# The last 64 channels of an MLP computed with tokens on partitions, and the last output tile stored in three parts

## The chip, the cores and the metric

One core of a Trainium2 chip runs the whole program. The metric is the device time in microseconds (us) of one execution. The profiler's span is 1.3 to 1.6 us shorter than the time that the same execution is given.

## The reference

A transformer block with adaptive modulation: attention with 32 heads over a cache of 2048 keys, then a gated sub-block whose MLP has 1728 inner channels. Only that MLP is touched.

```python
# x: (1, 2048, 640); w3: (640, 1728); w4: (1728, 640)
h = _gelu(_layernorm(x, axis=-1) @ w1)
hs = jnp.concatenate([g0, g1, g2, g3], axis=-1) @ w2   # g0..g3: quarters of h, shifted along the tokens
x1 = x + hs
h2 = _gelu(_layernorm(x1, axis=-1) @ w3) @ w4
return x1 + h2
# and outside:
x = x + gb * _B_ref(h, B_w1, B_w2, B_w3, B_w4)
```

1728 is 13 x 128 + 64, so the last tile of inner channels is half full.

## The kernel before

The program is written as a list of operations. A scheduler with a cost model puts them in order on each engine, and the result is one fixed instruction stream per engine. It decides with this line how long an engine is taken:

```python
t_eng[e] = s + (o.dur if o.dma else max(o.dur - self.LAP.get(e, 0.0), 60.0))
```

The W3 product puts 128 inner channels on partitions and 512 tokens in the free dimension; the 14th tile is padded with zero weights. W4 then takes gelu's output as the stationary operand, 128 tokens at a time.

```python
def w3_part(ch, key):
    for f in range(NF):                        # NF = 14
        m = Tile(pool="T")
        for kk in range(KT):                   # KT = 5
            P.op("PE", ... matmul(m.ap, w3_ap[:, kk, f * 128:(f + 1) * 128], nT_ap[ch][:, kk, :], ...)   # 128 x 512
        P.op("ACT", ... activation(gT_ap[:, f, :], m.ap, GELU) ...)

def w4_tile(t, key):
    for hf in range(2):                        # two column halves of 320
        for f in range(NF):
            P.op("PE", ... matmul(m[:, hf * 512:hf * 512 + HD], gT_ap[:, f, i * 128:(i + 1) * 128],
                                  w4_ap[f][:, hf * HD:(hf + 1) * HD], ...)
        if last:                               # the last tile: each half is finished and stored by itself
            P.op("DVE", ... tensor_tensor(out=w[:, c0:c1], in0=m[...], in1=mod_t[5][:, c0:c1], op=ALU.mult) ...)
            P.op("DVE", ... tensor_tensor(out=o_[:, c0:c1], in0=w[:, c0:c1], in1=b[:, c0:c1], op=ALU.add) ...)
            dma("SP", ... dma_start(out2d[t * 128:(t + 1) * 128, c0:c1], o_[:, c0:c1]) ...)
```

The zeros are written by two fills, whose place in the order is set by a priority (`E + 12` is that of a stage near the end of attention, where the cache buffers under W3 and W4 come free):

```python
pad, pad2 = T(), T()
P.op("POOL", lambda e: e.memset(w3_ap[:, :, FF:FP], 0.0), 300, (), (pad,), E + 12, over=kv(2, 3, 4))
P.op("DVE", lambda e: e.memset(w4_ap[NF - 1][FL:128, :], 0.0), 400, (), (pad2,), E + 12, slack=500.0, over=kv(4))
```

In the same stretch the MLP's input is normalised. Here the vector engine reads two operands from SBUF (the on-chip memory that holds these tiles), while GpSimd does other multiplies and adds of the same stage:

```python
P.op("DVE", lambda e, ...: e.scalar_tensor_tensor(            # "the centring"
    out=b.ap, in0=x1[t].ap, scalar=mv_ap[g1][:, i, 0:1], in1=mod_t[4][:], op0=ALU.subtract, op1=ALU.mult), ...)
...
tt("POOL", b.ap, b.ap, mod_t[3][:], ALU.add, ...)
```

## Time and profile before

| | before |
|---|---|
| time, median of 3 runs (range) | 1368.05 us (1367.85 to 1371.74) |
| last query projection but one to first W1 matmul | 26.58 us (1170.47 to 1197.05) |
| first W1 to first W3 matmul | 30.28 us |
| W3 and W4 stretch, first W3 to end of last matmul | 139.10 us |
| last matmul to last vector instruction, and on to the end | 1.05 and 1.82 us |

The segments come from the trace in order of time. The first W3 matmul of the kernel before is missing from its trace; its start is taken as 0.216 us ahead of the first one recorded. The marker at 1170.47 is the last query projection but one (one more begins 11.31 us later). The page gives the span to 0.1 us, so every length that is reckoned to the end of the run, here and in the tables below, is good to 0.05 us only. A row has the start in us, the duration in us, the engine (SPq is the queue that issues transfers), the line, the operation, output and inputs, shapes, a count, and in brackets the idle time before it with what ended it.

GpSimd in order of time, near the end of attention:

```profile
1177.15 1.56 POOL L538 TENSOR_TENSOR f_y<-f_y,f_mod 128x640 f32<-128x640 f32 x1
1178.66 1.54 POOL L538 TENSOR_TENSOR f_hT<-f_tmp,f_y 128x640 bf16<-128x640 f32 x1
1181.30 0.36 POOL L921 MEMSET f_KV<- 128x320 bf16 x1 [1.10 <-PE f_O L825]
1182.70 1.54 POOL L538 TENSOR_TENSOR f_hT<-f_tmp,f_y 128x640 bf16<-128x640 f32 x1 [1.03 <-DVE f_rl L832]
```

The vector engine in order of time, the same microseconds:

```profile
1178.98 1.91 DVE L861 SCALAR_TENSOR_TENSOR f_y<-f_hT,f_small,f_mod 128x640 f32<-128x640 bf16 x1
1182.82 0.33 DVE L922 MEMSET f_KV<- 64x320 uint32 x1
...
1187.14 0.86 DVE L861 SCALAR_TENSOR_TENSOR f_y<-f_hT,f_small,f_mod 128x640 f32<-128x640 bf16 x1
```

GpSimd works without a break until 1180.20. Then its fill has to wait 1.10 us for the matmuls that still read the buffer. One centring lasts 1.91 us where its peers last 0.86: it starts at 1178.98.

### The profile page before, as it was taken

What the parts mean: (1) busy time and instruction counts of PE and PEld (TensorE: products, weight loads), DVE (VectorE), ACT (ScalarE), POOL (GpSimd) and SP (SyncE); (2) the same over time, 40 slices, a digit from 0 to 9 for tenths busy, and PEclk for the clock granted to TensorE, in tenths of its full rate; (3) what the DMA queues carried; (4) which work ended last, traced back from release to release, by engine and by line L of the source; (5) the groups of instructions that cost most, each with busy time, mean ns of one, the idle gap of its engine ahead of it and who ended that gap; (6) DMA issues with size and microseconds to landing.
All of it is one profiled execution on the core that took longest, in us unless ns stands there. A gap on an engine that the chain in (4) does not pass through costs nothing.

```text
span 1369.3 us, 29631 instructions
## 1 busy us (share of the span) xinstructions
PE 1349.0 (99%) x12841; PEld 939.4 (69%) x13075; DVE 574.7 (42%) x1440; ACT 1103.3 (81%) x1145; POOL 111.7 (8%) x97
## 2 busy tenths in 40 slices
PE   8999999999999999999999999999999999999999
PEld 6666777677677777677677777776776776655665
DVE  5554344544323332332333233233233345799553
ACT  6988888888888888888888888888888888833322
POOL 1000000000000000000000000000233237500000
PEclk9999999999999999999999999999999999999999
DMA  9642614272335221241205121422236110441210
GB/s 211 144 97 36 115 40 81 34 130 59 81 65 90 55 48 35 48 89 33 58 10 101 36 47 36 91 54 48 55 63 136 27 15 19 114 84 44 40 43 31
DMA packets 264787, 90.38 MB, mean 66 GB/s; under 512 B 244793, under 2 KB 262266, under 8 KB 264650
## 3 DMA queue, kind: packets, MB, share of 16 engines
q1 hardware_dynamic: 260682, 84.17, 30.9%
q0 software_dynamic: 672, 2.56, 0.9%
q10 hardware_dynamic: 3296, 1.67, 0.6%
q8 instruction: 104, 1.70, 0.5%
q14 instruction: 33, 0.27, 0.1%
HBM read 41.68 MB, written 2.63 MB: 32 GB/s over the span
## 4 chain that ended last, share of the span: by engine, by line
PE 96%; DMA 1%; issue 1%; DVE 1%; ACT 0%; POOL 0%; SPq 0%; POOLq 0%
PE f_O L825 35%; PE f_S L806 29%; PE f_M L729 10%; PE f_M L760 10%; PE f_S L1002 2%; PE f_M L1002 2%; PE f_O L989 2%; PE f_S L989 2%; PE f_S L940 1%; PE f_S L963 1%; PE f_M L963 1%; DMA f_KV<-in_A_v_cache_dram 1%; PE f_O L940 1%; DMA f_W<-in_w_mod_dram 1%; PE f_O L760 0%
## 5 line engine op out<-in xcount | busy, mean ns | idle before, releaser
L808 ACT ACTIVATE f_PQ<-f_S 128x1024 bf16<-128x1024 f32 x1024 | 1042.6, 1024 | 137.5 <-PE f_S L806 105.0
L825 PEld LDWEIGHTS f_O<-f_KV,f_PQ 128*128 128x128 bf16 x8192 | 634.8, 98 | 262.3 <-DVE f_small L517 1.4
L825 PE MATMUL f_O<-f_KV,f_PQ 128*128 128x129 bf16 x8192 | 796.4, 220 | 9.3 <-DMA f_KV<-in_A_v_cache_dram 0.9
L806 PE MATMUL f_S<-f_PQ,f_KV 128*128 128x512 bf16 x1831 | 650.8, 379 | 3.2 <-DMA f_KV<-in_A_k_cache_dram 0.7
L768 DVE TENSOR_TENSOR f_y<-f_M,f_y 128x320 f32<-128x320 f32 x192 | 94.4, 492 | 465.5 <-PE f_M L760 465.5
L760 PE MATMUL f_M<-f_wo,f_OO 128*128 128x320 bf16 x992 | 272.9, 299 | 0.0
L806 PEld LDWEIGHTS f_S<-f_PQ,f_KV 128*128 128x128 bf16 x2048 | 191.6, 98 | 13.4 <-ACT f_PQ L808 2.2
L729 PE MATMUL f_M<-f_hT,f_wq 128*128 128x512 bf16 (+1 forms) x635 | 189.0, 378 | 1.8 <-DVE f_tmp L771 0.2
L760 PEld LDWEIGHTS f_M<-f_wo,f_OO 128*128 128x128 bf16 x992 | 96.3, 98 | 28.5
L834 DVE TENSOR_TENSOR f_OO<-f_O,f_rl 128x256 bf16<-128x256 f32 x256 | 108.4, 423 | 8.3
L538 POOL TENSOR_TENSOR f_y<-f_y,f_mod 128x640 f32<-128x640 f32 x32 | 49.2, 1544 | 735.2 <-DVE f_y L768 735.1
L733 DVE CAST f_PQ<-f_M 128x512 bf16<-128x512 f32 x127 | 87.8, 692 | 50.7 <-PE f_M L729 49.5
L729 PEld LDWEIGHTS f_M<-f_hT,f_wq 128*128 128x128 bf16 x640 | 62.5, 98 | 49.8 <-DVE f_tmp L771 0.6
L832 DVE RECIPROCAL f_rl<-f_O 128x2 f32<-128x2 f32 x256 | 43.5, 170 | 69.1 <-PE f_O L825 58.2
L992 ACT ACTIVATE f_OO<-f_S 128x512 bf16<-128x512 f32 x28 | 16.7, 597 | 43.6 <-PE f_S L989 43.6
L766 DVE COPY f_y<-f_M 128x320 f32<-128x320 f32 x32 | 15.7, 492 | 57.6 <-PE f_M L760 57.6
L499 DVE BATCH_NORM_STATS2 f_small<-f_y 128x6 f32<-128x320 f32 (+1 forms) x72 | 32.3, 479 | 1.0 <-POOL f_y L538 0.9
L1002 PE MATMUL f_S<-f_KV,f_OO 128*128 128x320 bf16 x224 | 31.7, 299 | 0.0
L1002 PE MATMUL f_M<-f_KV,f_OO 128*128 128x320 bf16 x224 | 31.7, 299 | 0.0
L544 ACT ACTIVATE f_xn<-f_y,f_small 128x640 bf16<-128x640 f32 x10 | 9.1, 916 | 25.7 <-DVE f_small L523 25.7
L661 DVE TENSOR_REDUCE f_small<-f_tmp 128x1 f32<-128x640 f32 x20 | 16.4, 820 | 29.9 <-ACT f_PQ L808 29.9
L992 ACT ACTIVATE f_OO<-f_O 128x512 bf16<-128x512 f32 x28 | 16.7, 596 | 14.1 <-PE f_O L989 14.1
(148 smaller groups left out, 534.9 us busy)
## 6 DMA issues: line engine op xcount, KB each, us to landing
f_KV<-in_A_v_cache_dram SPq DMA_DIRECT2D x28, 512.0 KB, 4.7
f_wo<-in_A_wo_dram SPq DMA_DIRECT2D x8, 640.0 KB, 4.3
f_wq<-in_A_wq_dram SPq DMA_DIRECT2D x7, 640.0 KB, 4.9
f_xin<-in_A_x_dram SPq DMA_DIRECT2D x13, 320.0 KB, 3.5
out_dram<-f_xin SPq DMA_DIRECT2D x15, 160.0 KB, 1.8
f_KV<-in_B_w_dram SPq DMA_DIRECT2D x5, 432.0 KB, 3.6
f_KV<-in_A_k_cache_dram SPq DMA_TRANSPOSE x128, 2.7
f_OO<-f_OO SPq DMA_TRANSPOSE x128, 2.5
```

The source lines that it names most:

```text
L538: P.op(eng, lambda e: e.tensor_tensor(out=out, in0=a, in1=b, op=op), COST[eng][0], rd, wr, prio, lat=300 if eng == "POOL" else None, dual= ...
L729: P.op("PE", lambda e, i=i, kk=kk, mm=mm, a=a, z=z: e.matmul(mm[:, 0:z - a], wq_t[g % 2][:, kk, hh * 128:(hh + 1) * 128], hT_t[ch][:, kk, ...
L733: P.op("DVE", lambda e: e.tensor_copy(q.ap, m.ap), 690, (m,), (q,), s * NP - 90)
L760: P.op("PE", lambda e, m=m, qt=qt, hf=hf, hh=hh: e.matmul(m[:, 0:HD], OT_ap[gs][:, qt, hh, :], wo_t[g % 2][:, hh, hf * HD:(hf + 1) * HD], ...
L768: P.op("DVE", lambda e, m=m, yt=yt: e.tensor_tensor(out=yt.ap, in0=m[:, 0:HD], in1=yt.ap, op=ALU.add), 490, (m, yt), (yt,), s * NP - 60)
L806: P.op("PE", lambda e, sp=sp, r=r, kt=kt: e.matmul(sp[:, r * QC:(r + 1) * QC], K_ap[b][:, kt * 128:(kt + 1) * 128], q.ap, start=True, stop ...
L808: x = P.op("ACT", lambda e, sp=sp, pt=pt: e.activation(pt.ap.rearrange("p k q -> p (k q)"), sp.ap, ACT.Exp, scale=SCALE), 1021, (sp,), (pt ...
L825: ins = e.matmul(o[bk][:, w * 129:w * 129 + 129], pt[:, r, qt * 128:(qt + 1) * 128], V_ap[b][:, u, 0:129], start=(u == 0 and w == 0), stop ...
L832: P.op("DVE", lambda e, ov=ov, i0=i0: e.reciprocal(rl_t[:, i0:i0 + 2].unsqueeze(2), ov[:, 0:258].rearrange("p (u d) -> p u d", u=2)[:, :, ...
L834: evac.append(P.op("DVE", lambda e, ov=ov, i0=i0, bk=bk: e.tensor_tensor(out=On_ap[gs][:, 2 * bk:2 * bk + 2, hh, :], in0=ov[:, 0:258].rear ...
L989: P.op("PE", lambda e, m=m, f=f, kk=kk: e.matmul(m.ap, w3_ap[:, kk, f * 128:(f + 1) * 128], nT_ap[ch][:, kk, :], start=(kk == 0), stop=(kk ...
L1002: P.op("PE", lambda e, f=f, hf=hf: e.matmul(m[:, hf * 512:hf * 512 + HD], gT_ap[:, f, i * 128:(i + 1) * 128], w4_ap[f][:, hf * HD:(hf + 1) ...
```

## The change

The intent is to stop computing the 64 padded channels, and to shorten what follows the last matmul. The last 64 channels are computed with tokens on partitions (64 columns instead of a full 128 x 512 tile), gelu is applied, and a DMA transpose turns them. Two token tiles share one turned tile, so W4 gets a second copy of its last weights, with the zeros in the other half. The last output tile is finished in parts of 320, 192 and 128 columns. The scheduler may now let matrix operations last less than 60 ns.

```diff
@@ the scheduler
-            t_eng[e] = s + (o.dur if o.dma else max(o.dur - self.LAP.get(e, 0.0), 60.0))
+            t_eng[e] = s + (o.dur if o.dma or e == "PE" else max(o.dur - self.LAP.get(e, 0.0), 60.0))
@@ the fills
-    pad, pad2 = T(), T()
-    P.op("POOL", lambda e: e.memset(w3_ap[:, :, FF:FP], 0.0), 300, (), (pad,), E + 12, over=kv(2, 3, 4))
-    P.op("DVE", lambda e: e.memset(w4_ap[NF - 1][FL:128, :], 0.0), 400, (), (pad2,), E + 12, slack=500.0, over=kv(4))
... (cut: the old load of the last weights)
+    w4b = T(), T()
+    for i in range(2):
+        w = w4_ap[NF - 1 + i]
+        P.op("POOL", lambda e, w=w: e.memset(w, 0.0), 700, (), (w4b[i],), 3000, over=kv(4))
+        dma("SP", lambda e, i=i, w=w: e.dma_start(w[i * FL:(i + 1) * FL, :], B_w4[(NF - 1) * 128:FF, :]), 80, (), (w4b[i],), E + 10)
@@ w3_part
+        m = Tile(pool="T")
+        for kk in range(KT):
+            for i in range(4):
+                c0 = (i % 2) * 128 + (i // 2) * FL
+                P.op("PE", ... e.matmul(m[:, c0:c0 + FL], nT_ap[ch][:, kk, i * 128:(i + 1) * 128], w3_ap[:, kk, FN * 128:FF], ...)
+        P.op("ACT", lambda e, m=m: e.activation(gl_ap, m[:, 0:256], GELU), act(256), (m,), (gl,), key, over=old)
+        dmaT(lambda e: e.dma_start_transpose(gT_ap[:, FN, 0:256].rearrange("p (k q) -> p k q", k=2), gl_ap), 64, (gl,), (gT[FN],), key, over=old)
-        for f in range(NF):
+        for f in range(FN):                                  # 13 full tiles
@@ w4_tile
-        for hf in range(2):
+        if last:
+            m3 = Tile(pool="T")
+            parts = ((m, 0, 0, HD), (m, 512, HD, 512), (m3, 0, 512, D))
+        else:
+            parts = ((m, 0, 0, HD), (m, 512, HD, D))
... (cut: the loops over these parts)
```

One thing moves beside what the words name: both fills are now GpSimd's, at priority 3000, so behind the additions of that stage.

More of the change, by code (lines that the diff above doesn't have):

```diff
@@ L287, in fast_path @@
     FL = FF - (NF - 1) * 128
-    FP = NF * 128
+    FN = NF - 1
     G4 = D // 4
@@ L360, in fast_path @@
     gT = [T() for _ in range(NF)]
+    gl_ap = gT_ap[:, NF - 1, 256:512]
+    gl = T()
     wq = [[T() for _ in range(HG)] for _ in range(2)]
@@ L379, in fast_path @@
     W3_OFF = 2 * KVW
-    w3_ap = KV_t[:, W3_OFF:W3_OFF + KT * FP].rearrange("p (k n) -> p k n", k=KT)
+    w3_ap = KV_t[:, W3_OFF:W3_OFF + KT * FF].rearrange("p (k n) -> p k n", k=KT)
     w3 = [T() for _ in range(KT)]
-    W4_HI = W3_OFF + KT * FP
+    W4_HI = W3_OFF + KT * FF
     NW4 = 12
-    w4_ap = [KV_t[:, f * D:(f + 1) * D] for f in range(NW4)] + [KV_t[:, W4_HI + f * D:W4_HI + (f + 1) * D] for f in range(NF - NW4)]
+    w4_ap = [KV_t[:, f * D:(f + 1) * D] for f in range(NW4)] + [KV_t[:, W4_HI + f * D:W4_HI + (f + 1) * D] for f in range(NF + 1 - NW4)]
     w4 = [T() for _ in range(3)]
     w4_of = lambda f: w4[0] if f < 6 else (w4[1] if f < NW4 else w4[2])
-    assert NW4 * D <= W3_OFF and W4_HI + (NF - NW4) * D <= NKV * KVW
+    assert NW4 * D <= W3_OFF and W4_HI + (NF + 1 - NW4) * D <= NKV * KVW and FL == 64
     MM = lambda n: n / 2.4 + 2.5
@@ L910, in fast_path @@
     for k, old in ((0, kv(2)), (1, kv(2)), (2, kv(2, 3)), (3, kv(3)), (4, kv(3, 4))):
-        dma("SP", lambda e, k=k: e.dma_start(w3_ap[:, k, 0:FF], B_w3[k * 128:(k + 1) * 128, :]), 432, (), (w3[k],), E + 5 + k, over=old)
+        dma("SP", lambda e, k=k: e.dma_start(w3_ap[:, k, :], B_w3[k * 128:(k + 1) * 128, :]), 432, (), (w3[k],), E + 5 + k, over=old)
     for i, (f0, f1, old) in enumerate(((0, 6, kv(0)), (6, 12, kv(0, 1)))):
@@ L916, in fast_path @@
     dma("SP", lambda e: e.dma_start(w4_ap[NF - 2], B_w4[(NF - 2) * 128:(NF - 1) * 128, :]), 160, (), (w4[2],), E + 10, over=kv(4))
-    w4b = T()
-    dma("SP", lambda e: e.dma_start(w4_ap[NF - 1][0:FL, :], B_w4[(NF - 1) * 128:FF, :]), 80, (), (w4b,), E + 10, over=kv(4))
-    pad, pad2 = T(), T()
-    P.op("POOL", lambda e: e.memset(w3_ap[:, :, FF:FP], 0.0), 300, (), (pad,), E + 12, over=kv(2, 3, 4))
-    P.op("DVE", lambda e: e.memset(w4_ap[NF - 1][FL:128, :], 0.0), 400, (), (pad2,), E + 12, slack=500.0, over=kv(4))
+    w4b = T(), T()
[3 more added lines that the diff above has]
+        dma("SP", lambda e, i=i, w=w: e.dma_start(w[i * FL:(i + 1) * FL, :], B_w4[(NF - 1) * 128:FF, :]), 80, (), (w4b[i],), E + 10)
     DEL = [1, -1, 2, -2]
@@ L985, in w3_part @@
     def w3_part(ch, key):
-        for f in range(NF):
+        old = tuple(a for b in On + OT for a in b) if ch == 0 else ()
+        m = Tile(pool="T")
+        for kk in range(KT):
+            for i in range(4):
+                c0 = (i % 2) * 128 + (i // 2) * FL
+                P.op("PE", lambda e, m=m, kk=kk, i=i, c0=c0: e.matmul(m[:, c0:c0 + FL], nT_ap[ch][:, kk, i * 128:(i + 1) * 128], w3_ap[:, kk, FN * 128:FF],
+                                                                     start=(kk == 0 and i == 0), stop=(kk == KT - 1), skip_group_check=True),
+                     MM(FL) + 4, (w3[kk], nT[ch][i]), (m,), key + 0.1 * kk + 0.01 * i, accum=True)
+        P.op("ACT", lambda e, m=m: e.activation(gl_ap, m[:, 0:256], GELU), act(256), (m,), (gl,), key, over=old)
+        dmaT(lambda e: e.dma_start_transpose(gT_ap[:, FN, 0:256].rearrange("p (k q) -> p k q", k=2), gl_ap), 64, (gl,), (gT[FN],), key, over=old)
+        for f in range(FN):
             m = Tile(pool="T")
@@ L990, in w3_part @@
                                                                     start=(kk == 0), stop=(kk == KT - 1)),
-                     MM(QC), (w3[kk], pad) + tuple(nT[ch]), (m,), key + f + 0.1 * kk, accum=True)
+                     MM(QC), (w3[kk],) + tuple(nT[ch]), (m,), key + 1 + f + 0.1 * kk, accum=True)
             P.op("ACT", lambda e, m=m, f=f: e.activation(gT_ap[:, f, :], m.ap, GELU),
-                 act(QC), (m,), (gT[f],), key + f, over=tuple(a for b in On + OT for a in b) if ch == 0 else ())
+                 act(QC), (m,), (gT[f],), key + 1 + f, over=old)
     def w4_tile(t, key):
@@ L999, in w4_tile @@
         last = t == SQ // 128 - 1
-        for hf in range(2):
+        if last:
[3 more added lines that the diff above has]
+            parts = ((m, 0, 0, HD), (m, 512, HD, D))
+        for n, (mm, o, c0, c1) in enumerate(parts):
             for f in range(NF):
-                P.op("PE", lambda e, f=f, hf=hf: e.matmul(m[:, hf * 512:hf * 512 + HD], gT_ap[:, f, i * 128:(i + 1) * 128],
-                                                                 w4_ap[f][:, hf * HD:(hf + 1) * HD], start=(f == 0), stop=(f == NF - 1)),
-                     MM(HD), (gT[f], w4_of(f), w4b, pad2), (m,), key + hf + 0.01 * f, accum=True)
+                P.op("PE", lambda e, f=f, mm=mm, o=o, c0=c0, c1=c1: e.matmul(mm[:, o:o + c1 - c0], gT_ap[:, f, (i % 2 if f == FN else i) * 128:][:, 0:128],
+                                                                             w4_ap[f + i // 2 if f == FN else f][:, c0:c1], start=(f == 0), stop=(f == NF - 1)),
+                     MM(c1 - c0), (gT[f],) + ((w4b[i // 2],) if f == FN else (w4_of(f),)), (mm,), key + n + 0.01 * f, accum=True)
             if last:
-                c0, c1 = hf * HD, (hf + 1) * HD
-                w, o_ = tmp[t % 2], xin[3 * hf]
-                P.op("DVE", lambda e, hf=hf, c0=c0, c1=c1: e.tensor_tensor(out=w[:, c0:c1], in0=m[:, hf * 512:hf * 512 + HD], in1=mod_t[5][:, c0:c1], op=ALU.mult),
-                     490, (m, mod[5][hf]), (w,), key - 1000)
-                P.op("DVE", lambda e, o_=o_, c0=c0, c1=c1: e.tensor_tensor(out=o_[:, c0:c1], in0=w[:, c0:c1], in1=b[:, c0:c1], op=ALU.add), 490, (w, b), (o_,), key)
+                w, o_ = tmp[t % 2], xin[(0, 3, 1)[n]]
+                P.op("DVE", lambda e, mm=mm, o=o, c0=c0, c1=c1: e.tensor_tensor(out=w[:, c0:c1], in0=mm[:, o:o + c1 - c0], in1=mod_t[5][:, c0:c1], op=ALU.mult),
+                     dve(c1 - c0), (mm,) + tuple(mod[5]), (w,), key - 1000)
+                P.op("DVE", lambda e, o_=o_, c0=c0, c1=c1: e.tensor_tensor(out=o_[:, c0:c1], in0=w[:, c0:c1], in1=b[:, c0:c1], op=ALU.add),
+                     dve(c1 - c0), (w, b), (o_,), key)
                 dma("SP", lambda e, o_=o_, c0=c0, c1=c1: e.dma_start(out2d[t * 128:(t + 1) * 128, c0:c1], o_[:, c0:c1]), 80, (o_,), (), key)
```

## The prediction

> **What bounds the kernel now.** I read the page first, then the chain that ended last over the closing part, then the matrix engine in order of time, then the head (where small matmuls can be seen alone), then the last six microseconds. The page gives the engine shares:
>
> ```profile
> PE 1349.0 (99%) x12841; PEld 939.4 (69%) x13075; DVE 574.7 (42%) x1440; ACT 1103.3 (81%) x1145; POOL 111.7 (8%) x97
> PE 96%; DMA 1%; issue 1%; DVE 1%; ACT 0%; POOL 0%; SPq 0%; POOLq 0%
> ```
>
> The first line is busy time; the second is the chain of waits that ends the run. Both say the matmul stream is the limit, with the clock at 1.00 throughout. The diff touches only the MLP at the end, so what counts is whether that stretch is also matmul-bound. The chain from the fourth W3 chunk to the end (start, length, what):
>
> ```profile
> 1336.16 2.10 PE f_S L989 x9
> 1338.26 2.16 PE f_O L989 x10
> ...
> 1358.82 3.80 PE f_M L1002 x28
> 1362.62 3.82 PE f_S L1002 x28
> 1366.44 0.02 issue
> 1366.46 0.50 DVE f_tmp L1008
> 1366.97 0.02 issue
> 1366.99 0.49 DVE f_xin L1010
> ```
>
> Line 989 is the W3 product, line 1002 the W4 product. They follow each other with no gap, so time taken off a matmul there moves everything behind it. Ten 512-column matmuls take 2.16 us, so one is 0.216 us; 28 320-column ones take 3.80 us, so one is 0.136 us. (The missing tenth record at 1336 is lost, not a wait: 9 x 0.216 is only 1.94 us.) After the last matmul only a multiply, an add and the store remain.
>
> Small matmuls, each with a full 128x128 weight load of its own, are visible in two places: the modulation columns in the head and the attention's PV products. In order of time (start, length, engine):
>
> ```profile
> 9.29 0.65 PE L465 MATMUL f_M<-f_s_bf,f_W 128*128 128x1 bf16 x20 [0.16 <-DMA f_W<-in_w_mod_dram]
> 9.28 0.56 PEld L465 LDWEIGHTS f_M<-f_s_bf,f_W 128*128 128x128 bf16 x20 [0.30 <-DMA f_W<-in_w_mod_dram]
> 1177.59 0.66 PEld L825 LDWEIGHTS f_O<-f_KV,f_PQ 128*128 128x128 bf16 x8
> 1177.80 0.62 PE L825 MATMUL f_O<-f_KV,f_PQ 128*128 128x129 bf16 x8
> ```
>
> A record of a matmul includes its drain (0.16 us for one column, the mean of that group; 0.22 us for 129). So 20 one-column matmuls start (0.65 - 0.16) / 19 = 26 ns apart, and their 20 loads (0.56 - 0.10) / 19 = 24 ns apart. The eight PV matmuls start (0.62 - 0.22) / 7 = 57 ns apart. A load for every matmul is therefore no more than some 25 ns, and at 129 columns it is wholly hidden.
>
> [...]
>
> **The change part by part.**
>
> (1) W3, last 64 channels. Removed per 512-token chunk: five 512-column matmuls on a half-empty tile, 5 x 0.216 = 1.08 us. Added: 5 x 4 matmuls with 128 tokens stationary and 64 weight columns moving. [...]I allow 31 ns: 20 x 31 = 0.62 us. Saved 0.46 us per chunk, 4 chunks, **1.84 us**, all of it on the chain. W4 keeps its 14 products per column half: the two token tiles turned together share one 128-row stationary block, and two weight tiles with zeros in opposite halves pick the right one. Nothing is saved or lost there.
>
> (2) The turn by DMA. Gelu now covers 256 columns instead of 512 for this tile (ACT is far from bound here: in the first W3 window, 1227.3 to 1242.6, it is busy 8.46 of 15.30 us). Then one DMA transpose; existing transposes land 2.6 to 2.7 us after issue. It is computed first in the chunk, and 13 tiles x 1.08 = 14 us of W3 work follow before W4 needs it, as its last product. So **0 us** on the path, four times.
>
> (3) Zero fills. The vector-engine memset of 0.33 us at 1182.82 goes away; the chain runs through it there, but the only visible wait of the matrix engine is 0.26 us on the attention eviction behind it. The GpSimd memset of 0.36 us becomes two of 640 columns, by size about 0.7 us each, in a spot where GpSimd idles 1.03 us. I count **0.2 us** gained.
>
> (4) The last output tile in 320 + 192 + 128 columns. Matmuls: 14 x (136 + 82.5 + 56) = 3.84 us against 14 x 272 = 3.80, a loss of 0.04. After the last matmul the two vector operations cover 128 instead of 320 columns[...], so 0.40 us gained. The middle part's multiply and add (about 0.36 + 0.36) just fit into the 0.78 us in which the last part's matmuls run. The final store is 32 KB instead of 80 KB, but still 128 rows, now of 256 B; I count 0.05 us. Together **0.4 us**.
>
> (5) The scheduler's own model now lets matrix operations last under 60 ns. That changes computed times, and so the order of instructions on the other engines. The head transposes are affected by only 2 ns each. I count 0, with a spread.
>
> Sum: 1.84 + 0.2 + 0.4 = 2.4 us, rounded up slightly for unequal chunks: 1368.05 - 2.5 = **1365.5 us**, 0.2% faster.
>
> **The rivals.**
>
> Load-bound small matmuls. If load and matmul do not overlap at 64 columns, each costs 24 + 29 = 53 ns, 20 cost 1.06 us, and part 1 saves nothing: about 1367.4.[...]
>
> A wait for the turned tile. The transposes share the SP queue[...]. In the wait view the queue waited up to 14.2 us for one vector result in this stretch; if the new transpose stood behind such a wait, W4's last product would wait. The slack of 14 us makes one or two microseconds, not more, and I hold it unlikely: 1366 to 1369.
>
> The vector engine takes over. In the first W3 window it is busy 15.02 of 15.30 us. If matmuls arrive 0.46 us earlier, the W2 eviction behind could come late. But at 1244.00 it had idled 0.50 us waiting for the matrix engine, so it had caught up. If it does bind, chunk 0's gain is lost: 0.5 us.
>
> A shifted order near the end of attention, where between 1168 and 1197 matmuls, exponentials and evictions interlock: one bad collision like the 1.91 us vector instruction at 1178.98 (its peers take 0.88) would cost or give 1 us.
>
> **Range and chances.** The matmul gain is known to about 0.5 us, the rest has about 1 us of spread, and the three runs before already span 1367.85 to 1371.74, skewed upwards. So 8 times in 10 between 1363.6 and 1368.4. Two per cent is 27 us; the entire W3 part that is touched is 4 x 1.08 us, so faster by 2% cannot come from this, and slower would need a stall repeated through the attention. Faster 0.004, same 0.988, slower 0.008.
>
> **What would show it.** Twenty 64-column matmuls of a chunk in about 0.62 us, starting 29 to 33 ns apart (step 1); 53 ns or more proves the first rival. No matrix wait on a DMA in front of the first W4 tile of each chunk (step 2); a wait there proves the second. Four W3 stretches of about 14.65 us instead of 15.1. From last matmul to last vector instruction about 0.62 us instead of 1.04 (step 4). If the gain in the MLP is there but the end of attention starts the MLP earlier or later than 1197.05, that difference is steps 3 and 5. The prediction is wrong if such a shift exceeds 2 us, or if the small matmuls are load-bound.

The lengths used here for shapes that the kernel before doesn't have can be estimated from its trace. For matmuls, 136 ns at 320 columns and 216 at 512 are 0.417 ns a column; carried on in a straight line that is 29 ns at 64, 83 at 192 and 56 at 128 (at 129, 57 are measured). For the vector engine's multiplies and adds, 492 ns at 320 columns and 824 at 640 are 1.04 ns a column, which leaves 359 ns at 192 and 293 at 128. From issue to landing, the trace's groups of transposes have medians of 2.5 to 2.7 us, but for two smaller groups with 3.4 and 4.0.

## More of the kernel before

At the end each queue leaves the main stream by a branch, reads a guard's flag, and branches again, past a general version of the kernel that isn't needed.

The transfer queue in order of time, the two stores of the last tile:

```profile
1365.61 1.04 SPq L1011 DMA_DIRECT2D out_dram<-f_xin  x1
...
1367.51 0.33 SPq L1011 DMA_DIRECT2D out_dram<-f_xin  x1
```

The first issue takes three times as long as the second. Nobody waits for it; the second one ends the run.

## The result

| | before | changed |
|---|---|---|
| median (range) of 4 runs each, same rounds | 1367.97 us (1367.85 to 1371.74) | 1369.27 us (1367.79 to 1370.63) |
| ratio, 95% interval | | 1.0003 (0.9982 to 1.0023) |
| last query projection but one to first W1 | 26.58 us | 27.57 us |
| first W1 to first W3 | 30.28 us | 30.68 us |
| W3 and W4 stretch | 139.10 us | 137.14 us |
| last matmul to last vector instruction | 1.05 us | 0.73 us |
| last vector instruction to end | 1.82 us | 2.04 us |

A ratio is the mean time of one kernel's runs over that of the other's of the same rounds, so it isn't quite the ratio of the medians quoted beside it. All outputs are right.

The five segments sum to 198.83 us before and 198.16 us after, 0.67 us less. Both traced runs nevertheless have a span of 1369.3 us, because the changed kernel's last query projection but one happened to begin 0.67 us later. That is chance in the head, the first 100 us of the program: in the 14 traces a scalar-engine activation (f_tmp<-f_nTx) starts anywhere between 94.0 and 99.7 us (at 97.40 and at 94.19 in the two traces of the changed kernel), and from there to the first GpSimd multiply of the late stage it is 858.61 or 858.62 us in every one. The first three segments, on the other hand, came out within 0.03 us whenever a kernel's order in them was unchanged. I compare segments, therefore, and take the times as a check. The gain of 1.96 us in the MLP is there. It was given back ahead of it.

The page of the changed kernel, its line of busy time and its line of the chain of waits; then the pieces of that chain at the end (start, length, what):

```profile
PE 1347.6 (98%) x12915; PEld 940.5 (69%) x13149; DVE 577.0 (42%) x1441; ACT 1103.2 (81%) x1145; POOL 111.7 (8%) x98
PE 95%; DMA 2%; DVE 1%; issue 1%; ACT 0%; POOL 0%; SPq 0%; POOLq 0%; DVEq 0%
```

```profile
1358.89 3.80 PE f_M L1021 x28
1362.70 3.06 PE f_S L1021 x28
1365.75 0.80 PE f_O L1021 x14
```

The bound hasn't changed, and the last part's 14 matmuls take 0.80 us.

The matrix engine of the changed kernel in order of time, each chunk's small group and the first full tile behind it:

```profile
1229.39 0.75 PE L994 MATMUL f_S<-f_KV,f_wq 128*128 128x64 bf16 x20
1230.19 1.03 PE L1002 MATMUL f_O<-f_wq,f_KV 128*128 128x512 bf16 x4
...
1261.93 0.75 PE L994 MATMUL f_S<-f_KV,f_wo 128*128 128x64 bf16 x20
...
1306.68 0.75 PE L994 MATMUL f_O<-f_KV,f_wq 128*128 128x64 bf16 x20
...
1336.51 0.75 PE L994 MATMUL f_S<-f_KV,f_nTx 128*128 128x64 bf16 x20
```

All four groups take 0.75 us with the drain; less some 0.19 us of it (between the 0.16 of one column and the 0.22 of 129) the 20 start 0.56 / 19 = 29 ns apart. The wait view of the matrix engine over the whole stretch is empty: no turned tile was waited for.

GpSimd of the changed kernel in order of time:

```profile
1177.82 1.54 POOL L541 TENSOR_TENSOR f_y<-f_y,f_mod 128x640 f32<-128x640 f32 x1
1179.31 1.55 POOL L541 TENSOR_TENSOR f_hT<-f_tmp,f_y 128x640 bf16<-128x640 f32 x1
1180.82 1.53 POOL L541 TENSOR_TENSOR f_y<-f_y,f_mod 128x640 f32<-128x640 f32 x1
1184.85 1.54 POOL L541 TENSOR_TENSOR f_hT<-f_tmp,f_y 128x640 bf16<-128x640 f32 x1 [2.49 <-DVE f_rl L835]
1186.33 1.20 POOL L924 MEMSET f_KV<- 128x640 bf16 x2
```

The vector engine, the same centring:

```profile
1179.65 3.40 DVE L864 SCALAR_TENSOR_TENSOR f_y<-f_hT,f_small,f_mod 128x640 f32<-128x640 bf16 x1
```

The fill no longer stands between two GpSimd instructions, so they follow each other without a gap. The centring that starts in the first of them ends 0.70 us after the second one has ended (1182.35), 1.49 us longer than before. The rule "length = what is left of GpSimd's work + 0.68 to 0.70 us" fits this centring in all 14 traces, with 1.2 us of work left or 2.7. The centring that ran beside a fill, which reads nothing, wasn't lengthened: at 1187.21 in the changed kernel 0.32 us of a fill were left, and it took 0.87 us. GpSimd's own instructions beside the long centring took 1.53 to 1.55 us, as the others do. So I read the lengths in this way: the centring got through only once GpSimd's tensor operations had ended, and the second of these started while the centring was already waiting, and wasn't held up for it. The traces show the lengths; what brings them is not shown. The long instruction lies on the path that sets the end, as the chain of waits of the changed kernel shows (before, this piece was 1.82 us):

```profile
1179.73 3.31 DVE f_y L864
1183.04 0.40 DVE f_tmp L774
```

What follows it are the evictions (the vector engine takes finished sums out of PSUM, the memory that matmuls write to) that the matrix engine waits for.

A second wait, 0.40 us, is between W1 and W3. The matrix engine in order of time, before and then changed, at two W2 products:

```profile
1212.16 1.52 PE L963 MATMUL f_S<-f_W,f_PQ 128*128 128x320 bf16 x10
1213.52 1.52 PE L963 MATMUL f_M<-f_W,f_PQ 128*128 128x320 bf16 x10
```

```profile
1213.82 1.52 PE L966 MATMUL f_S<-f_W,f_PQ 128*128 128x320 bf16 x10
1215.56 1.53 PE L966 MATMUL f_M<-f_W,f_PQ 128*128 128x320 bf16 x10 [0.22 <-DVE f_y L969]
```

The second product starts 1.74 us after the first instead of 1.36, because its PSUM tile hasn't been evicted yet. The stretch has the same work, in another order on the vector engine.

At the very end, the changed kernel's vector engine and its transfer queue in order of time:

```profile
1366.64 0.29 DVE L1026 TENSOR_TENSOR f_tmp<-f_O,f_mod 128x128 f32<-128x128 f32 x1
1366.97 0.29 DVE L1028 TENSOR_TENSOR f_xin<-f_tmp,f_y 128x128 bf16<-128x128 f32 x1
```

```profile
1365.68 0.33 SPq L1030 DMA_DIRECT2D out_dram<-f_xin  x1
...
1367.29 0.75 SPq L1030 DMA_DIRECT2D out_dram<-f_xin  x1
```

The two vector instructions take 0.29 us each, as the estimate from the trace of before had it (293 ns). But the long issue, which was the first of two before, is now the last, and the end comes later for it.

### The profile page after: what moved, and what is told of

It is laid out like the page before. It is cut to its first block, busy times and chain, and to the rows that moved or that the text cites. A ratio compares the mean times of both kernels' runs of the same rounds, so it can differ in the third digit from the quotient of the medians.

```text
span 1369.3 us, 29785 instructions
## 1 busy us (share of the span) xinstructions
PE 1347.6 (98%) x12915; PEld 940.5 (69%) x13149; DVE 577.0 (42%) x1441; ACT 1103.2 (81%) x1145; POOL 111.7 (8%) x98
## 4 chain that ended last, share of the span: by engine, by line
PE 95%; DMA 2%; DVE 1%; issue 1%; ACT 0%; POOL 0%; SPq 0%; POOLq 0%; DVEq 0%
PE f_O L828 35%; PE f_S L809 28%; PE f_M L732 10%; PE f_M L763 10%; PE f_M L1021 2%; PE f_S L1021 2%; PE f_O L1002 2%; PE f_S L1002 2%; DMA f_KV<-in_A_v_cache_dram 1%; PE f_S L943 1%; PE f_M L966 1%; PE f_S L966 1%; PE f_O L943 0%; DMA f_hT<-f_xn 0%; DMA f_W<-in_w_mod_dram 0%
## 5 line engine op out<-in xcount | busy, mean ns | idle before, releaser
L1021 PE MATMUL f_S<-f_KV,f_OO 128*128 128x320 bf16 (+1 forms) x224 | 31.0, 296 | 0.0
L1021 PEld LDWEIGHTS f_M<-f_KV,f_OO 128*128 128x128 bf16 x224 | 21.9, 98 | 8.9
L1021 PEld LDWEIGHTS f_S<-f_KV,f_OO 128*128 128x128 bf16 x224 | 21.7, 98 | 8.2
```

The lines of the kernel that those rows point to most:

```text
L1021: P.op("PE", lambda e, f=f, mm=mm, o=o, c0=c0, c1=c1: e.matmul(mm[:, o:o + c1 - c0], gT_ap[:, f, (i % 2 if f == FN else i) * 128:][:, 0:12 ...
```

## The experiments

Theory A: the placement of the fills cost about 1.4 us, by the lengthened centring and by the changed order behind it, and hid the gain in the MLP. Rival B: the scheduler's new rule shifted the order. Rival C: the MLP gain is real, but the small group or its turn costs elsewhere. Question D: why did the last store gain nothing? Twelve runs were made. This table has what they measured; "q" is the last query projection but one, ratios are against the kernel before in the same rounds, and the segments come from each run's trace.

| run | median us (runs) | ratio (95%) | q to W1 | W1 to W3 | W3 and W4 | last matmul to end |
|---|---|---|---|---|---|---|
| before | 1369.11, 1367.91, 1369.02, 1369.56, 1369.37 (9 each) | | 26.58 | 30.28 | 139.10 | 2.87 |
| changed | 1369.27 (4) | 1.0003 (0.9982 to 1.0023) | 27.57 | 30.68 | 137.14 | 2.77 |
| after_again | 1367.61 (5) | 0.9994 (0.9981 to 1.0008) | 27.55 | 30.68 | 137.15 | 2.60 |
| fills_late | 1372.29 (5) | 1.0018 (1.0004 to 1.0031) | 27.55 | 30.68 | 139.10 | 2.85 |
| fills_as_before | 1366.55 (5) | 0.9983 (0.997 to 0.9997) | 26.57 | 30.28 | 137.14 | 3.05 |
| clamp_only | 1370.41 (5) | 1.0003 (0.999 to 1.0017) | 26.56 | 30.28 | 139.10 | 2.88 |
| gap_by_wait | 1366.67 (4) | 0.9986 (0.9971 to 1.0001) | 26.26 | 30.68 | 137.14 | 3.12 |
| group_last | 1371.2 (4) | 1.0015 (0.9999 to 1.003) | 26.57 | 30.27 | 139.63 | 3.17 |
| two_halves | 1368.33 (4) | 0.9995 (0.998 to 1.001) | 26.55 | 30.28 | 137.12 | 2.94 |
| last_store_act | 1369.87 (5) | 1.001 (0.9996 to 1.0024) | 26.57 | 30.28 | 137.14 | 4.52 |
| w3_loads_split | 1368.81 (5) | 0.9989 (0.9974 to 1.0003) | 26.55 | 30.28 | 137.14 | 3.07 |
| w4_loads_split | 1366.2 (5) | 0.9981 (0.9967 to 0.9996) | 26.55 | 30.28 | 137.15 | 3.01 |
| fewer_fillers | 1370.71 (5) | 1.001 (0.9996 to 1.0023) | q to W3: 56.83 | | 137.14 | 2.66 |
| flag_early | 1368.1 (5) | 0.9987 (0.9974 to 1.0001) | q to W3: 56.86 | | 137.14 | 2.96 |

In the last two traces the record of the very first W1 matmul, missing in all others, is there, so only the sum of the two segments can be compared (56.86 before). The five medians of before: the first for after_again, fills_late, fills_as_before and clamp_only, the second for gap_by_wait to last_store_act, the third for the two splits, then one each.

**The changed kernel again.** To have the spread, and a second trace.

> The changed kernel again, for a tighter ratio on the same chip and a second trace. Order theory: 0 to 1 us from before, the long scalar-tensor-tensor of over 3 us in the trace again. Chance theory: that instruction is 1 to 2 us long this time and the kernel is 2 us faster than before.

The first three segments came out as in the first trace to 0.03 us, the median 1.66 us lower. That difference is the head's. What does differ is the last issue, 0.61 us instead of 0.75.

**Only the fills' placement, on the kernel before.**

```diff
-    P.op("POOL", lambda e: e.memset(w3_ap[:, :, FF:FP], 0.0), 300, (), (pad,), E + 12, over=kv(2, 3, 4))
-    P.op("DVE", lambda e: e.memset(w4_ap[NF - 1][FL:128, :], 0.0), 400, (), (pad2,), E + 12, slack=500.0, over=kv(4))
+    P.op("POOL", lambda e: e.memset(w3_ap[:, :, FF:FP], 0.0), 300, (), (pad,), 3000, over=kv(2, 3, 4))
+    P.op("POOL", lambda e: e.memset(w4_ap[NF - 1], 0.0), 700, (), (pad2,), 3000, over=kv(4))
... (cut: the load of the last weights now follows the fill)
```

> The kernel before with only the placing of the zero fills taken from the change: both on GpSimd, after its other work (W3, W4 and the last tile as before). Order theory: the two GpSimd tensor operations then follow each other without a break, the vector engine's scalar-tensor-tensor beside them takes over 3 us as in the changed kernel (1.9 us before), and the time rises by 1.4 to 2.2 us over the kernel before, with nothing gained elsewhere. Rival theory, that the lost gain is chance between executions or is lost in the first microseconds: within 0.4 us of before.

The vector engine of this run in order of time:

```profile
1179.33 3.38 DVE L861 SCALAR_TENSOR_TENSOR f_y<-f_hT,f_small,f_mod 128x640 f32<-128x640 bf16 x1
```

The long centring, the 27.55 us and the 30.68 us are all there without any of the rest of the change, and the kernel is slower than before by 0.18%. This run shows that the placement costs (27.55 - 26.58) + (30.68 - 30.28) = 1.37 us.

**The whole change, with the fills placed as before** (GpSimd's at priority E + 12, the other one on the vector engine).

```diff
-        P.op("POOL", lambda e, w=w: e.memset(w, 0.0), 700, (), (w4b[i],), 3000, over=kv(4))
+    P.op("POOL", lambda e: e.memset(w4_ap[NF][0:FL, :], 0.0), 300, (), (w4z[1],), E + 12, over=kv(2, 3, 4))
+    P.op("DVE", lambda e: e.memset(w4_ap[NF - 1][FL:128, :], 0.0), 400, (), (w4z[0],), E + 12, slack=500.0, over=kv(4))
... (cut: the loads no longer follow the fills; W4 waits for load and fill)
```

> The whole change, but its zero fills placed as the kernel before has them (one on GpSimd between its tensor operations, one on the vector engine). Order theory: the stretch before the MLP is as in the kernel before, and the MLP's gain of some 2 us and the end's 0.3 shows: 2.0 to 2.6 us faster than before. Chance or head theory: no faster than the changed kernel, within 0.5 us of before.

GpSimd and then the vector engine of this run in order of time:

```profile
1178.59 0.62 POOL L923 MEMSET f_KV<- 64x640 bf16 x1 [1.11 <-PE f_O L828]
```

```profile
1176.27 1.89 DVE L864 SCALAR_TENSOR_TENSOR f_y<-f_hT,f_small,f_mod 128x640 f32<-128x640 bf16 x1
```

The fill waits for the matrix engine as it did before, the centring is short again, and both segments are back. The ratio is 0.9983 with an interval below 1: this is a version that beats the kernel before and, in its rounds, was 1.06 us below the changed kernel's median. With fills_late it settles theory A from both sides. Rival C falls too: the group and its turn are all there, and no segment is longer than before except the last.

**Only the scheduler's rule, on the kernel before** (the first two lines of the diff above).

> The kernel before with only the scheduler's rule for short matrix operations changed; it reorders five vector-engine instructions near the beginning and nothing else. Theory that this reorder costs the 0.65 us by which the changed kernel's trace was already late at 1160 us: 0.5 to 0.8 us slower than before. Order theory (the reorder is harmless): within 0.2 us.

Five early vector instructions change places, and no segment changes by more than 0.02 us. Rival B falls.

**The gap, without the fill that made it.** In the changed kernel, GpSimd's second instruction of the pair is made to wait for the centring. No fill is moved.

```diff
-                    P.op("DVE", lambda e, b=xb[t], ...: e.scalar_tensor_tensor(
+                    centred[t] = P.op("DVE", lambda e, b=xb[t], ...: e.scalar_tensor_tensor(
...
-                    tt("POOL", b.ap, b.ap, mod_t[3][:], ALU.add, (b,) + tuple(mod[3]), (b,), prio)
+                    tt("POOL", b.ap, b.ap, mod_t[3][:], ALU.add, (b,) + tuple(mod[3]), (b,), prio, need=(lambda: centred[8],) if t == 7 else ())
... (cut: the helper tt hands the wait on)
```

> The changed kernel (zero fills late on GpSimd) with one wait added: GpSimd's second tensor operation of the pair waits until the vector engine's first scalar-tensor-tensor of that stage is done. Theory that the loss is this one collision[...]: that instruction takes about 1.9 us instead of 3.4, and the stretch from the last query projection to the MLP's first matmul 26.2 to 26.6 us instead of 27.55; the further 0.40 us between there and the first W3 product stay if they come from the changed vector order, and go if they come from the collision. Rival, that the fills' own time on GpSimd or the loss of the vector fill's place is to blame: 27.5 us as in the changed kernel.

GpSimd and then the vector engine of this run in order of time:

```profile
1180.37 1.54 POOL L541 TENSOR_TENSOR f_y<-f_y,f_mod 128x640 f32<-128x640 f32 x1 [0.76 <-DVE f_y L866]
```

```profile
1178.41 1.88 DVE L866 SCALAR_TENSOR_TENSOR f_y<-f_hT,f_small,f_mod 128x640 f32<-128x640 bf16 x1
```

One wait on GpSimd took 1.31 us off the segment (27.57 to 26.26), with the traces' order of vector, scalar and GpSimd instructions the same as in the changed kernel. So running beside GpSimd's second instruction is the cause; that the centring stands still meanwhile is read from the lengths above. The 26.26 us are 0.31 below fills_as_before. The vector engine's fill, through which the chain of waits of the kernel before ran for 0.34 us, is gone, and that is the likely reason, the part of the prediction's third step that held; but the vector engine's order differs between these two as well, so it isn't isolated. The 0.40 us between W1 and W3 stayed. Fills_late shows that the fills' placement brings it, and this run that it isn't the long centring; which swap in the vector engine's order makes it I haven't separated.

**The 64-channel group last in its chunk instead of first.**

```diff
-                      ... MM(FL) + 4, (w3[kk], nT[ch][i]), (m,), key + 0.1 * kk + 0.01 * i, accum=True)
+                      ... MM(FL) + 4, (w3[kk], nT[ch][i]), (m,), key + 20 + 0.1 * kk + 0.01 * i, accum=True)
```

(and the activation and the turn behind it in the same way; based on the kernel with fills as before)

> The run fills_as_before with the 64-channel group computed as the last tile of each chunk instead of the first (same work, same results). Theory that its transpose is hidden only by the 14 us of matmuls behind it: about 0.5 us of gelu and handover and some 2.5 us from issue to landing now stand before the fourteenth W4 product, of which 1.8 us (13 x 0.136) are covered, and 1.4 us more in the two chunks with a W2 tile between: 1 to 2 us of matrix wait in each of two or three chunks, 3 to 6 us slower in all. Rival: the transpose costs nothing in either place, within 0.5 us of fills_as_before.

The wait view of the matrix engine over the MLP has one line in this run (who waited, for what: total us, times, longest):

```profile
PE f_M L1023 <- DMA f_OO<-f_OO: 2.1, 2, 1.1
```

The stretch is 2.49 us longer, so the turn is not free anywhere: it is free because the group comes first and 13 full tiles follow it. Less was lost than expected, since two of the four chunks had other matmuls to put in between.

**The last tile in two halves** (based on the kernel with fills as before).

```diff
-            parts = ((m, 0, 0, HD), (m, 512, HD, 512), (m3, 0, 512, D))
+            parts = ((m, 0, 0, HD), (m, 512, HD, D))
```

> The run fills_as_before with the last output tile in two halves of 320 columns as in the kernel before. What the three parts are worth: from the last matmul to the last vector instruction 1.05 us again instead of 0.73, from there to the end 1.8 us if the long issue again falls on the first of the two stores, up to 2.5 if on the last. Prediction's step 4 (worth 0.4 us) against the reading of the traces (worth between -0.2 and 0.4, depending on where the long issue falls).

From the last matmul to the end it is 2.94 us with halves. With three parts nine traces have 2.60 to 3.17, mean 2.94 (last_store_act left out). The kernels that leave the last tile as it was (before, fills_late and clamp_only) have 2.85 to 2.88. So no gain of three parts is to be seen in this spread, though the vector engine is done 0.32 us sooner; some 0.3 us must be lost in the store.

**The last store from the scalar engine's queue.**

```diff
-                dma("SP", ...
+                dma("ACT" if n == 2 else "SP", ...
```

> The run fills_as_before with one difference: the third, last part of the output is stored by the scalar engine's queue instead of the sync engine's. Theory: in the changed kernel the last issue on the sync queue takes 0.61 to 1.04 us instead of 0.33 because it waits for a 16 KB instruction fetch that runs at that moment; from another queue the last issue is not held up, and the time from the last vector instruction to the end falls from 1.88 to 2.32 us to 1.6 to 1.7. Rival: rows of 256 bytes are slow to store[...]; then the time stays at 1.9 us or more.

A miss, and the most instructive one. The issue was short (0.37 us), but the store landed 3.00 us after the last matmul, against 2.91 with fills as before, and the scalar queue, which now had to stay in the program for it, read the guard's flag at 3.90 and branched at 4.41 us: 1.5 us lost. So it isn't the SP queue's issue alone that is slow. Nor are the short rows, going by the packets: in the changed kernel the stores' packets of 256, 384 and 640 B took 18, 22 and 32 ns (medians).

The trace's records of single packets show what is. Near the end of each run one instruction fetch of 16,384 bytes lasts 0.9 to 1.7 us. The records don't name a packet's DMA engine, but of the 128 rows of a store just 8 are held up by it, which is one engine's share of the 16 that the page counts; so I take it that the fetch occupies one of the 16 DMA engines. Of every store that meets the fetch, 120 rows are through within some 0.4 us, and the other 8 come one after another once the fetch is over. With fills as before the fetch lasts from -0.07 to 1.42 us (from the last matmul's end): the last rows of the first store land between 1.4 and 1.9, of the second between 2.0 and 2.1, and the third store's issue, begun at 0.75, ends at 1.79, 0.37 us after the fetch. In all 13 traces with an SP issue under way when the fetch ends, that issue ends 0.29 to 0.38 us after it. The end of the run follows as well: in the nine traces with three parts and all stores on the SP queue the fetch ends anywhere from 1.05 to 1.52 us after the last matmul, and the run 1.57 to 1.65 us after the fetch. Before the change the fetch lasts from -1.51 to -0.14; it makes the first of two issues long and is over long before the last.

**Five or two more transfers on the SP queue.** The first theory of the fetch was that it is the SP queue's own, at a fixed place in its stream, so that a longer stream moves it.

```diff
-        dma("SP", lambda e, k=k: e.dma_start(w3_ap[:, k, :], B_w3[k * 128:(k + 1) * 128, :]), 432, (), (w3[k],), E + 5 + k, over=old)
+        [dma("SP", lambda e, k=k, p=p: e.dma_start(w3_ap[p * 64:(p + 1) * 64, k, :], ...), 216, ...) for p in range(2)]
```

> The changed kernel with the zero fills as before, and each of the five W3 loads split into two of 64 rows: five more issues on the SP queue, the same bytes, the order of all other engines unchanged. If the long last issue (0.6 to 1.15 us instead of 0.33) comes from the fetch of 16 KB of instructions at a fixed place of that queue's stream, the fetch moves to another issue: the last one takes 0.33 us, and last vector instruction to end is about 1.65 us instead of 2.32; median about 0.6 us below the kernel with fills as before. If the third store is slow for a reason of its own, the last issue stays at 0.6 us or more. All earlier segments as in the kernel with fills as before (26.57, 30.28, 137.14).

```diff
-    for i, (f0, f1, old) in enumerate(((0, 6, kv(0)), (6, 12, kv(0, 1)))):
+    for i, (f0, f1, old) in enumerate(((0, 3, kv(0)), (3, 6, kv(0)), (6, 9, kv(0, 1)), (9, 12, kv(0, 1)))):
```

> The same kernel with the two 960 KB W4 loads split into two each: two more issues instead of five. If the fetch follows the place in the stream, it falls one or two issues earlier against the stores than with fills as before: on the first or second of the last three stores, where it is hidden, last issue 0.33 us, 1.65 to 1.9 us from last vector instruction to end. If it does not follow the place, nothing changes (2.3 us).

The last issue of the run with split W3 loads, in order of time:

```profile
1365.59 1.11 SPq L1032 DMA_DIRECT2D out_dram<-f_xin  x1
```

Neither moved it: the last issue took 1.11 and 0.97 us. The theory fell. In the trace the matrix engine's queue leaves the program by branches just ahead of the fetch (the second one began 0.11 us before it in the kernel before, 0.13 in the changed one), which led to the next two runs.

**Fewer filler matmuls in the head.** The matrix engine's own stream made 80 instructions shorter, to take away another 16 KB fetch some 6 us before the end that might hold that queue up.

```diff
-        P.op("PE", lambda e: dummy(e, n, t), n * 56, (ones,), (t,), key)
+        P.op("PE", lambda e: dummy(e, 6 if n == 26 else n, t), n * 56, (ones,), (t,), key)
...
-                if k < 2:
-                    dummy(e, 1)
```

> The changed kernel with the zero fills as before and 40 of the head's filler matmuls left out (80 instructions fewer, with their weight loads, in the matrix engine's stream; the order of all other engines unchanged). The two splits refuted that the late 16 KB fetch hangs on a place in the SP stream. In all twelve traces it starts 0.10 to 0.12 us after the last branch of the matrix engine's queue, and the store issue that is under way ends 0.30 to 0.38 us after the fetch. New theory: that branch comes late in the changed kernels because another 16 KB of the matrix engine's own stream had to be fetched some 6 us before the end; in the kernel before that fetch lies 15 us before the end and the branch 1.6 us before the last matmul's end. 80 instructions at 3.80 us per 56 are 5.4 us, so the earlier fetch should fall past the end and vanish: branch about 3.9 us before the end, fetch over before the last issue, last issue 0.33 us, last vector instruction to end 1.65 to 1.85 us instead of 2.32. Rival: the last of three stores is slow whatever the fetch does: issue over 0.6 us, 2.1 us or more. The head may change by its own luck; 26.57, 30.28 and 137.14 us stay.

The earlier fetch vanished as foreseen (the one before last is now 18.6 us before the last packet), but the last one stayed: it began 0.12 us after the last matmul's end, took 0.93 us, and the last issue took 0.68 us. Half of the theory was right, and not the half that mattered.

**The guard's flag read before the last 42 matmuls.**

```diff
+            if e == "PE":
+                run(e, n, late)                     # late: all but the last 42
+                eng.wait_ge(self.flag_op.sem, self.flag_op.semval)
+                eng.load(redo[eng.engine], flag[0:1, 0:1])
... (cut: the rest of the stream; this queue's later read is left out)
```

> The changed kernel with the zero fills as before, and the matrix engine's queue reads the guard's flag before the last 42 matmuls instead of after them; the schedule is otherwise the same. What the run with fewer fillers left: the earlier fetch vanished as foreseen, but the last branch stayed late (0.29 us before the last matmul's end) and the last issue long (0.68 us), so the earlier fetch is not the cause. In all traces the queue has handed out its last matmul 2.59 us before the end of the last 320-column part, but only 1.25 us before that of a 128-column part; then it reads the flag and takes the branch out of the program about 1 us later, and the 16 KB fetch follows 0.05 to 0.41 us after. Theory: with the flag read already, the branch comes about 1.2 us before the last matmul's end, the fetch of 0.9 to 1.7 us is over before or soon after the second store's issue, the last issue (0.75 us after the last matmul) takes 0.33 us, and last vector instruction to end is 1.65 to 1.85 us instead of 2.32; 137.14 us for the W3 and W4 stretch stay, as the queue is some 20 matmuls ahead when it reads the flag. Median 0.5 us below the kernel with fills as before, so about 2.8 us below the kernel before. Rival: the last issue stays at 0.6 us or more although the fetch is over: then the fetch is not what holds it.

The second branch moved, from 0.19 to 0.74 us before the last matmul's end, but the fetch did not: -0.05 us, against -0.07. The last issue took 0.93 us. So the fetch doesn't follow the second branch. It follows the first one, from the main stream over the general version of the kernel: 1.08 to 1.21 us after it in twelve traces, 1.37 with fewer fillers and 2.30 in two halves. Counted from that branch's end it is 0.71 to 0.75 us in all but fewer fillers (1.00): in two halves the branch itself took 1.57 us, elsewhere 0.37 to 0.46. The matrix engine's queue takes that first branch 2.59 us before the end of the last matmul where the last part has 320 columns, and 1.25 us where it has 128, because it is some 20 matmuls ahead in both (my estimate: 2.59 / 0.136 = 19 and 1.25 / 0.056 = 22) and the shorter ones take less time. On this reading that is why a shorter last part brings the fetch under the last store. That the fetch delays the stores is shown by the packets and issues of the traces; that the first branch brings it is only read from their timing, since no run moved that branch by itself.

## Why the prediction was right, and where it was not

The same within 2% was right, and was safe: what the change touches is far smaller than 27 us. The time was not: 1365.5 us were predicted, 0.998 of before, and the ratio is 1.0003. The four plain runs' median of 1369.27 us lies above the range given, and after_again's 1367.61 inside it; which of the two comes out is the head's luck. The prediction's own sign for steps 3 and 5, an MLP that starts later although its gain is there, came true, with 1.39 us within the 2 us that it allowed. The steps:

- **Step 1, the matmul group, held.** 0.46 us per chunk was predicted, and 1.96 / 4 = 0.49 measured; 31 ns had been allowed for each small matmul, and 29 ns were needed. The load-bound rival (53 ns) fell; the 57 ns at 129 columns with a load for each had spoken against it.
- **Step 2, the hidden turn, held.** No wait of the matrix engine on a transfer appears in the MLP. Group_last shows the condition: it has to come early in the chunk (last in it, 2.49 us were lost).
- **Step 3, the zero fills, failed, and cancelled most of the gain.** It put a gain of 0.2 us on "a spot where GpSimd idles 1.03 us". It counted the fills as work and not as a spacer. Measured: 1.31 us lost by running beside GpSimd's second instruction, 0.40 us between W1 and W3, where the evictions come in another order, and some 0.3 us gained, most likely by the vector engine's missing fill; in all 1.39 us lost where 0.2 were to be gained (27.57 - 26.58 + 30.68 - 30.28). The last rival named this: "one bad collision like the 1.91 us vector instruction at 1178.98 (its peers take 0.88) would cost or give 1 us". The long instruction had been seen; what it waited for had not been asked, and so the change's move of the fill wasn't weighed against it.
- **Step 4, the last tile, was half right.** On the vector engine 0.32 us were gained where 0.40 were predicted. The two instructions are 0.20 us shorter each (0.29 instead of 0.49), as predicted, but the last multiply starts 0.11 us after the last matmul and not 0.03. The middle part's addition, which runs until 1366.54 (1366.18 + 0.36), is the likely reason: it doesn't quite "just fit". The store's 0.05 us had the wrong sign and size: from the last vector instruction to the end it took 0.06 to 0.62 us longer than before in the nine traces, and what it took follows the end of the instruction fetch, which the prediction didn't have.
- **Step 5, the scheduler's rule, held**: nothing.

The sum predicted was -2.4 us. The sum measured in the traced pair is -1.96 + 1.39 - 0.32 + 0.22 = -0.67 us, which the chance in the head, a few us between executions, hid in four runs. The prediction should have given that head more room in its range: the three runs before already showed it (1367.85 to 1371.74).

## What to carry to other kernels

An instruction that costs little can still be the spacer that keeps two engines out of each other's way, as the 0.36 us fill did here, whose move made a centring 1.49 us longer; before moving one, look at what runs on each side of it, and ask of every instruction in the profile that is twice as long as its peers what it is blocked by. Compare the segments between markers, which here agree to 0.03 us, before believing a difference of medians that the head's chance can make. Shortening the last piece of work can also change what runs under the last store (here a fetch that had ended 0.14 us before the last matmul's end, and then ended 1.05 to 1.52 us after it), so measure from the last matmul to the end, and not the vector engine alone. The version to keep is the change with the fills left where they were (0.9983).
